# A transformer block on one core: the order of the first layer norm, the background banks of the projections, and the transfer latencies of a build-time planner

## The chip, the cores and the metric

The kernel runs on one core of one Trainium2 chip. Its engines are TensorE (PE: matmuls, and PEld: weight loads), VectorE (DVE), ScalarE (ACT), GpSimd (POOL) and SyncE (SP), which here only issues transfers. The metric is device microseconds from start to end of one execution.

## The reference

One sequence of 2048 tokens of width 640 goes through a layer norm, an attention block of 32 heads of 20, a second layer norm and a gated block without an activation function:

```python
x = A_x                                                   # 2048 x 640, bfloat16
h = x + attention(layernorm(x) @ wqkv) @ wo               # 32 heads, Dh = 20, softmax over 2048 keys
n = layernorm(h)
h2 = h + ((n @ w_gate) * (n @ w_up)) @ w_down             # gate and up 640 -> 1728, down 1728 -> 640
```

Only the inputs `A_x`, `A_wqkv`, `A_wo`, `B_w_gate`, `B_w_up`, `B_w_down` are read; `B_x` is not used.

## The kernel before

**Tiles.** Tokens are 16 tiles of 128, in four blocks `b` of 512. Heads come in eight groups `g` of four; the heads of a group stand at 32-row steps of the array. Queries come in five chunks `ci` (`CHUNKS`: three of 512, two of 256). The unit of attention is one score bank: 128 keys by 512 queries of one head, with an exponential of it. There are 2048 such units, 64 for a group in a chunk of 512.

**A score bank's way.** `rows_into` (L989) computes scores from `KTt` and `QTt`. ScalarE takes three banks at a time from `SA` into `EA`, or two from `SB` into `EB` (L1064). VectorE takes a single bank from `D0` or `D1` into an integer tile `Y` (L1089), from which two more tiles come on VectorE (L1099) and a third on GpSimd (L1097); the four are bit patterns whose sum stands for the exponential. `emit_piece` (L1140) multiplies all of these with the values `VX` into the one accumulator bank `ACC`. When a group's 64 units are through, `close_group` copies `ACC` to `acs` (L1169), and the sums travel by four small transfers: `dscr<-acs`, `dn<-dscr`, a reciprocal on VectorE (L1173), `rscr<-rn`, and `bc<-rscr`, which spreads them over the partitions; GpSimd multiplies (L1198), and the result goes to `ON`.

**First layer norm.** `ln_block` calls `layer_norm` for block 0 (two halves of two tiles), then for blocks 1, 2 and 3. Blocks 0, 2 and 3 take their statistics on VectorE (L425, L427); block 1 takes them on ScalarE (L412: sums, L417: squares). Then two small ScalarE operations give the root (L431 and L432), VectorE takes the reciprocal (L433) and normalises (L450) into one of four tiles `t`. Blocks 0 and 1 are transposed on TensorE, with a copy to `LT` (in the tensor `R`); blocks 2 and 3 by DMA transposes (L466).

**Projections.** All other matmuls are background jobs: each holds one bank, and an `evac` operation empties it. Keys and queries of groups 0 and 1 are written by `direct_proj` straight to `KTt` and `QTt`. Those of groups 2 to 7 are computed densely, 120 features by 512 tokens a job (`dense`), copied to one of four tiles `QD` (in the tensors `HH` and `L`), written to DRAM (`kscr`, `qscr`), and read back to 32-row steps (`KTt<-kscr`, 512 KB, and `QT<-qscr`, 128 KB). There are four feature tiles `i`, each with four key jobs and one query job for the first chunk. Group 2 needs tile 0, group 3 tiles 0 and 1, group 5 tile 2, group 6 tiles 2 and 3. `v_proj` computes values, 160 features (two groups) by 128 tokens a job, emptied into `VX`. Later jobs are the output projection, the second layer norm and the gated block.

**What sets the order.** Everything is ordered when the program is built, by a planner with a clock of its own. Each operation has engines, a duration, a key (smaller goes first) and a latency `lat` until others see it. `try_start` gives a free engine the ready operation of smallest key; the order so found is the fixed order of that engine's instructions in the program. On the chip an engine that waits for an operand holds all behind it. Jobs have a `target`, a position in the stream of units, and are taken in the order of their targets if their operands are ready (`next_job`). `KLO` and `KHI` place the dense key and query jobs, by `g_list(64 * g_ + KLO, 64 * g_ + KHI, ...)`, with `g_` = 2, 3, 5, 6 for the four tiles. `take_bank` decides which bank a job may have: while attention runs, only one of `D0` and `D1` may hold a background job. `d_banks` gives `D` banks to VectorE's exponentials only once the last tile of `LT` is there. For a transfer the planner takes 0.6 us on SP and `DMA_LAT` until it has landed; only the first loads have a model with sizes (`load`).

Of the kernel before, what the change touches and what calls it, by code (L numbers as in the profile page):

```python
# [17 lines left out]
P = 128  # L18
# [13 lines left out]
LNPE = 2  # L32
LNACT = (1,)
GD = 2
CHUNKS = [(0, 512), (512, 512), (1024, 512), (1536, 256), (1792, 256)]
# [22 lines left out]
LAT = 0.12  # L58
DMA_LAT = 2.1
SWITCH = 0.105  # L60
# [81 lines left out]
def kernel(  # L142
# [200 lines left out]

    def dma(o, i, key, deps=(), dur=0.6, lat=DMA_LAT):
        return add("SP", dur, lambda e: nc.sync.dma_start(o, i), key, deps, lat=lat)

    with tc.manual_schedule():
# [6 lines left out]
        free["DVE"] = 1.5  # L354
        free["POOL"] = 6.0
        kdma = [0]

# [3 lines left out]

        landed = [0.0]

        def load(o, i, kb):

            def hook(t, end, e):
                landed[0] = max(landed[0], end + 1.4) + kb / 330.0
                op.lat = landed[0] - end
            op = dma(o, i, nk())
            op.hook = hook  # L370
            return op

# [11 lines left out]
        load_x(0, 0, 2)  # L384
        load_x(0, 2, 4)
        load_w("Q0", 0, 172)
        load_w("K0", 640, 812)
        load_x(1, 0, 4)
        load_w("V0", 1280, 1440)
# [4 lines left out]
        load_w("Q", 172, 640)  # L394
        wo_ops = [dma(WO[:, :, :], A_wo.rearrange("(c p) d -> p c d", p=P), 5000)]

# [4 lines left out]
        def layer_norm(tiles, key, tdeps, dst_of, tr_key, on_pe, front=False, on_act=False):  # L401
# [6 lines left out]
            if on_act:  # L408

                js = EA[0][:, 0:D]  # L410
                deps = ([prev] if prev is not None else [])
                sums = [add("ACT", 0.75, lambda e, i=i: nc.scalar.activation(js, tiles[i], ACT.Copy, accum_out=f4[:, 0, i:i + 1]),  # L412
                            (-1,), deps + [tdeps[i]]) for i in range(n)]
                ng = add("ACT", 0.2, lambda e: nc.scalar.mul(f4[:, 3, 0:n], f4[:, 0, 0:n], -1.0 / D), (-1,), sums)
                mean = add("DVE", 0.08, lambda e: nc.vector.tensor_scalar(mv[:, 0:n, 0], f4[:, 0, 0:n], scalar1=1.0 / D, scalar2=None,
                                                                         op0=ALU.mult), (key, n), sums)
                aggs = [mean] + [add("ACT", 0.75, lambda e, i=i: nc.scalar.activation(  # L417
                    js, tiles[i], ACT.Square, bias=f4[:, 3, i:i + 1], accum_out=mv[:, i, 1:2]), (-1,), [ng]) for i in range(n)]
                o2 = add("DVE", 0.08, lambda e: nc.vector.tensor_scalar(b4[:, 2, 0:n], mv[:, 0:n, 1], scalar1=1.0 / D, scalar2=EPS_B,
                                                                        op0=ALU.mult, op1=ALU.add), (key, n), aggs)  # L420
            else:
                aggs = []
                for i in range(n):
                    deps = [tdeps[i]] + ([prev] if prev is not None else [])
                    halves_ = [add("DVE", 0.41, lambda e, i=i, c=c: nc.vector.bn_stats(  # L425
                        st[:, i, c, :], tiles[i][:, c * 320:(c + 1) * 320]), (key, i), deps) for c in range(2)]
                    aggs.append(add("DVE", 0.13, lambda e, i=i: nc.vector.bn_aggr(mv[:, i, :], st[:, i, :, :]),  # L427
                                    (key, i, 1), halves_))
                o2 = add("DVE", 0.08, lambda e: nc.vector.tensor_scalar(b4[:, 2, 0:n], mv[:, 0:n, 1], scalar1=EPS_B, scalar2=None,
                                                                        op0=ALU.add), (key, n), aggs)  # L430
# [12 lines left out]
            for i in range(n):  # L443
# [5 lines left out]
                def fn(e, i=i, slot=slot):  # L449
                    nc.vector.tensor_scalar(slot["t"][1][:], tiles[i], scalar1=mv[:, i, 0:1], scalar2=f4[:, 2, i:i + 1],  # L450
                                            op0=ALU.subtract, op1=ALU.mult)
                a = add("DVE", 0.26, fn, (key, i, 2), [o6], lock=True, hook=hook, gate=lambda: bool(t6_free))
                if on_pe:
                    def evac(bank, pm, i=i, slot=slot):
                        release_later(now[0] + 0.3, lambda: t6_free.append(slot["t"]))
                        one_done(now[0])
                        src = bank.bitcast(BF16)[:, 0:D].rearrange("p (c k) -> p c k", c=KT)
                        return add(both(), c_psum(D), lambda e: copy_on(e, dst_of(i), src), EVK, [pm])
                    mms = [("T", c, slot) for c in range(KT)]
                    jb = make_job(mms, [a], evac, "D", front=front)  # L460
                    outs.append(jb.out)
                else:
                    def sent(t, end, e, slot=slot):
                        release_later(end + 2.2, lambda: t6_free.append(slot["t"]))
                        one_done(end)
                    outs.append(add("SP", 1.5, lambda e, i=i, slot=slot: nc.sync.dma_start_transpose(dst_of(i), slot["t"][1][:]),  # L466
                                    tr_key + i, [a], hook=sent, lat=2.2))
# [68 lines left out]
        def v_proj(p, t):  # L536
# [6 lines left out]
            def evac(bank, pm):  # L543
                o = VX[:, t, 8 * p * VS:(8 * p + 8) * VS].rearrange("p (h e) -> p h e", e=VS)[:, :, 0:Dh]
                return add(both(), c_psum(160), lambda e: copy_on(e, o, bank[:, 0:160].rearrange("p (h e) -> p h e", e=Dh)),
                           EVK, [pm])
            return make_job(mms, [wl["V" if p else "V0"], lt_ops[t]], evac)
# [4 lines left out]
        def dense(wname, col, w, b, dst):  # L552
# [6 lines left out]
            def evac(bank, pm):  # L559
# [3 lines left out]
                ev = add(both(), c_psum(512), lambda e: copy_on(e, QD[k][0:w, :], bank[0:w, :]), EVK, deps)  # L563
                d = dma(dst, QD[k][0:w, :], 6, [ev])
                qd_busy[k] = d
                after([d], lambda: finish(st, now[0]))
                return ev
            make_job(mms, [wl[wname], wl[wname + "0"]] + lt_ops[4 * b:4 * b + 4], evac)
            return st
# [29 lines left out]

        KLO, KHI, VLO, VHI = -120, -60, -60, 0  # L600

# [51 lines left out]
        def pad(scr, heads, c0, c1, key):  # L653

            z = GSt[0:96, 0:512]
            z = bass.AP(tensor=z.tensor, offset=z.offset, ap=[z.ap[0], [0, heads * 12 // 96], z.ap[1]])
            return dma(scr[:, c0:c1].rearrange("(h r) c -> h r c", r=32)[:, Dh:32, :], z, key, lt_ops, dur=1.4)

        zk = [pad(kscr, 4 * (NG - GD), b * 512, b * 512 + 512, 300) for b in range(4)]
        zq = [pad(qscr[b], H, 0, 512, 301 if b == 0 else 1000) for b in range(4)]  # L660
        for g in range(GD, NG):
            deps = [kst[i, b] for i in tiles_of(g, ktiles) for b in range(4)]
            op = dma(KTt[:, g, :], kscr[(g - GD) * P:(g - GD + 1) * P, :], 5, deps + zk)
            for b in range(4):
                kj[g, b] = [op]
        rows_done = {(ci, g): Mark() for ci in range(len(CHUNKS)) for g in range(NG)}
        for ci in range(len(CHUNKS)):
            q0, cw = CHUNKS[ci]
            b, off = q0 // 512, q0 % 512
            for g in range(NG):  # L670
# [4 lines left out]
                else:  # L675
                    deps = [qst[b, ft] for ft in tiles_of(g, qtiles)] + [rows_done[ci - 1, g]]
                qj[ci, g] = [dma(QTt[:, g, 0:cw], qscr[b][g * P:(g + 1) * P, off:off + cw],
                                 5 if ci == 0 else 7, deps + [zq[b]])]

# [3 lines left out]

        def weight(o, i, lat):

            op = dma(o, i, 1200, wq_prev, lat=lat)
            wq_prev[:] = [Mark()]
# [5 lines left out]
        for f0 in range(0, NF, 3):  # L693
            c0, c1 = f0 * P, min(f0 * P + 3 * P, FF)
            gl = [weight(W_[:, :, c0:c1], A_[:, c0:c1].rearrange("(c p) f -> p c f", p=P), 2.0 + 1.6)
                  for W_, A_ in ((WG, B_w_gate), (WU, B_w_up))]
            gl_ops += [gl] * 3
        wd_ops = [weight(WD[:, f0:f0 + 2, :], B_w_down[f0 * P:(f0 + 2) * P, :].rearrange("(f p) d -> p f d", p=P), 3.5)
                  for f0 in (0, 2)]

        wq_prev[:] = lt_ops
        for f0 in (4, 7, 10):
            wd_ops.append(weight(WD[:, f0:f0 + 3, :], B_w_down[f0 * P:(f0 + 3) * P, :].rearrange("(f p) d -> p f d", p=P), 3.6))
        wd_ops.append(weight(WD[0:64, 13, :], B_w_down[13 * P:FF, :], 2.5))

# [9 lines left out]
        def chunk_jobs(ci):  # L715
            q0, cw = CHUNKS[ci]
            wo_left = [2 * (cw // P)]
            for half in range(cw // 256):
# [3 lines left out]
                for tt in pair:  # L722
# [3 lines left out]
                    def xhook(t, end, e, xs=xs):  # L726
                        xs["t"] = t6_get()
                    row = q0 + tt * P
                    xop = add("SP", 0.6, lambda e, xs=xs, row=row: nc.sync.dma_start(xs["t"][1][:], x2d[row:row + P, :]),
                              1300 + ci, [mu_mark[ci, 4]], hook=xhook, gate=lambda: len(t6_free) > 1, lat=DMA_LAT)  # L730
                    for hf in range(2):
# [422 lines left out]
        def close_group(ci, g, end):  # L1154
# [15 lines left out]
            n = cw // 32  # L1170
            d1 = dma(dscr[d][0, 0:4 * cw].rearrange("(a q) -> a q", a=4), a[Dh:P:32, 0:cw], 10, [ev] + ([ds_use[d]] if ds_use[d] is not None else []))
            d2 = dma(DN[d][:, 0:n], dscr[d][0, 0:4 * cw].rearrange("(b c) -> b c", c=n), 10, [d1])
            rc = add("DVE", 0.07 + 0.0064 * n, lambda e: nc.vector.reciprocal(RN[d][:, 0:n], DN[d][:, 0:n]), (-2,), [d2])  # L1173
            d3 = dma(rscr[d][0, 0:4 * cw].rearrange("(b c) -> b c", c=n), RN[d][:, 0:n], 10, [rc])
            ds_use[d] = d3
            bdeps = [d3] + ([bc_use[0]] if bc_use[0] is not None else [])
            src = rscr[d][0:1, 0:4 * cw]
            bsrc = bass.AP(tensor=src.tensor, offset=src.offset, ap=[[cw, 4], [0, 32], [1, cw]])
            d4 = [dma(BC[0][:, 0:cw], bsrc, 10, bdeps)]

# [20 lines left out]
            def out_of(p0, f, m):  # L1201
                return add("SP", 0.6, lambda e: nc.sync.dma_start(ON[f % P:f % P + m, on_of[ci, f // P], 0:cw], o[p0:p0 + m, 0:cw]),  # L1202
                           (10,), [mu], lat=DMA_LAT)
# [16 lines left out]
        def take_bank():  # L1220
            bgs = sum(u == "bg" for u in bank_use["D"])
            for i in range(2):
                if bank_use["D"][i] is None and (bgs == 0 or not attn["started"] or attn["over"]):
                    return ("D", i)
# [311 lines left out]
```

The softmax here doesn't subtract the row's maximum and nothing guards it: scores larger than these inputs give would overflow.

## Time and profile before

| | |
|---|---|
| time | 892.97 us, median of 3 (891.44 to 893.55) |
| span of the profiled execution | 890.7 us |
| PE busy | 818.2 us (92%) |
| ACT busy | 763.0 us (86%) |
| DVE busy | 738.7 us (83%) |
| POOL busy | 347.8 us (39%) |
| first exponential on ACT starts | 24.10 us |
| last score, then only the rest of the gated block | about 820 us, to 890.7 us |

An engine's busy time includes its pipelined instructions, so a PE at 92% is not at its peak. Read the shares by stage: in the long middle three engines are busy nine tenths of the time or more, and an idle stretch of one of them means something only if the others have no work either. Times in the text are from the span's start.

### The profile page before, as it was taken

How to read it: one execution, taken by the hardware profiler on the slowest of the kernel's cores; microseconds unless marked ns; L12 is line 12 of the kernel's file. 1: busy time of each engine (PE TensorE's matmuls, PEld its weight loads, DVE VectorE, ACT ScalarE, POOL GpSimd, SP SyncE). 2: the span in 40 equal slices, each digit the busy share in tenths (PEclk: the TensorE clock that was granted, in tenths of full speed). 3: DMA queues.
4: the chain of work that ended last, by engine and by line, in shares of the span. 5: the costliest groups of instructions: out<-in, count | busy, mean ns of one | idle time of the engine just before them, and what ended most of it. 6: DMA issues, size and time to landing. Idle time of an engine off the chain costs nothing.

```text
span 890.7 us, 34291 instructions
## 1 busy us (share of the span) xinstructions
PE 818.2 (92%) x14496; PEld 394.4 (44%) x14496; DVE 738.7 (83%) x1987; ACT 763.0 (86%) x715; POOL 347.8 (39%) x516
## 2 busy tenths in 40 slices
PE   3998889979999899999999999999889999998988
PEld 2333334332333344444323444444355655655856
DVE  5587769879899989899999898988899998898343
ACT  5787779979998899999989999999899999998211
POOL 1023324435434444444554434434454544443100
PEclk9699799989999999999979999999899999999999
DMA  8463121222224431110101001010011111101100
GB/s 266 51 168 111 37 88 49 68 86 58 74 60 120 107 87 38 41 47 25 39 19 43 22 21 50 22 46 24 23 41 38 27 40 40 29 13 42 41 15 15
DMA packets 70441, 49.64 MB, mean 56 GB/s; under 512 B 33616, under 2 KB 66352, under 8 KB 70288
## 3 DMA queue, kind: packets, MB, share of 16 engines
q1 hardware_dynamic: 70288, 47.46, 19.7%
q8 instruction: 113, 1.85, 0.9%
q14 instruction: 40, 0.33, 0.1%
HBM read 30.88 MB, written 10.32 MB: 46 GB/s over the span
## 4 chain that ended last, share of the span: by engine, by line
PE 58%; DVE 21%; DMA 9%; ACT 5%; issue 4%; SPq 2%; POOL 1%; DVEq 0%; POOLq 0%; ACTq 0%
PE D L1313 20%; PE ACC L1140 16%; DVE Y L1089 8%; PE SA L989 6%; DVE Y L1099 6%; PE D L1290 6%; PE SB L989 5%; PE D L989 4%; ACT EA L1064 2%; DMA dn<-dscr 2%; DMA bc<-rscr 2%; SPq L1202 2%; ACT EB L1064 2%; DMA QT<-qscr 1%; DVE gs L323 1%
## 5 line engine op out<-in xcount | busy, mean ns | idle before, releaser
L1064 ACT ACTIVATE EA<-SA 128x1536 bf16<-128x1536 f32 x319 | 462.4, 1449 | 37.4 <-PE SA L989 17.6
L1097 POOL TENSOR_SCALAR Y<-Y 128x512 uint16<-128x512 uint16 x463 | 300.5, 649 | 406.2 <-DVE Y L1099 286.5
L1089 DVE TENSOR_SCALAR Y<-D 128x512 uint16<-128x512 f32 x463 | 315.1, 684 | 58.5 <-PE D L989 22.4
L1064 ACT ACTIVATE EB<-SB 128x1024 bf16<-128x1024 f32 x316 | 324.7, 1028 | 22.0 <-PE SB L989 12.1
L1140 PE MATMUL ACC<-Y,VX 128*32 128x512 bf16 (+1 forms) x2348 | 265.8, 344 | 10.2 <-DVE acs L1169 5.6
L1099 DVE TENSOR_SCALAR Y<-Y 128x512 uint16<-128x512 uint16 x926 | 258.6, 324 | 4.9 <-DVE Y L1089 0.5
L1140 PE MATMUL ACC<-EA,VX 128*32 128x512 bf16 (+1 forms) x1185 | 220.4, 349 | 1.4 <-ACT EA L1064 1.1
L989 PE MATMUL D<-QT,KTt 20*128 20x512 bf16 (+1 forms) x587 | 177.7, 342 | 11.5 <-DVE Y L1089 9.1
L1140 PE MATMUL ACC<-EB,VX 128*32 128x512 bf16 (+1 forms) x788 | 177.0, 349 | 0.0
L989 PEld LDWEIGHTS <-KTt 20*128 20x128 bf16 x2560 | 74.5, 92 | 227.4 <-issue 215.8
L1313 PEld LDWEIGHTS <-R 128*32 128x32 bf16 x5350 | 127.9, 98 | 97.1 <-issue 80.1
L1140 PEld LDWEIGHTS <-VX 128*32 128x32 bf16 x4321 | 119.5, 97 | 103.1 <-issue 82.8
L989 PE MATMUL SA<-QT,KTt 20*128 20x512 bf16 (+1 forms) x1185 | 132.9, 348 | 13.3 <-ACT EA L1064 7.7
L989 PE MATMUL SB<-QT,KTt 20*128 20x512 bf16 (+1 forms) x788 | 130.7, 348 | 1.3 <-ACT EB L1064 0.8
L1313 PE MATMUL D<-L,R 128*32 128x256 bf16 x3240 | 127.9, 274 | 3.7 <-DVE HH L823 1.7
L1313 PE MATMUL D<-R 128*32 128x160 bf16 (+1 forms) x2110 | 114.0, 314 | 5.6 <-DVE VX L323 3.1
L1198 POOL TENSOR_TENSOR os<-acs,bc 128x512 bf16<-128x512 f32 (+1 forms) x40 | 42.6, 1065 | 85.4 <-DMA bc<-rscr 37.2
L823 DVE TENSOR_TENSOR HH<-D,gs 128x256 bf16<-128x256 f32 x112 | 46.8, 417 | 21.3 <-ACT gs L321 20.6
L1313 PE MATMUL D<-R,HH 128*32 128x320 bf16 x1176 | 60.1, 301 | 1.4 <-DVE HH L823 1.0
L1313 PEld LDWEIGHTS <-HH 128*32 128x32 bf16 x1176 | 30.2, 96 | 21.2 <-issue 15.9
L321 ACT CAST gs<-D 128x256 bf16<-128x256 f32 (+1 forms) x28 | 10.4, 372 | 32.5 <-PE D L1290 32.5
L323 DVE CAST gs<-D 128x256 bf16<-128x256 f32 x84 | 34.6, 412 | 1.5 <-PE D L1313 1.1
(68 smaller groups left out, 350.5 us busy)
## 6 DMA issues: line engine op xcount, KB each, us to landing
bc<-rscr SPq DMA_DIRECT2D x24, 256.0 KB
KTt<-kscr SPq DMA_DIRECT2D x6, 512.0 KB
QT<-qscr SPq DMA_DIRECT2D x22, 128.0 KB
t<-in_A_x_dram SPq DMA_DIRECT2D x16, 160.0 KB
out_dram<-t SPq DMA_DIRECT2D x16, 160.0 KB
bc<-rscr SPq DMA_DIRECT2D x16, 128.0 KB
R<-in_B_w_gate_dram SPq DMA_DIRECT2D x4, 480.0 KB
R<-in_B_w_up_dram SPq DMA_DIRECT2D x4, 480.0 KB
```

The source lines that it names most:

```text
L323: nc.vector.tensor_copy(o, i)
L823: mu = add("DVE", c_psum(256), lambda e: nc.vector.tensor_tensor(HH[0:M, f, :], bank[0:M, 256:512], GS[k][0:M, :], ALU.mult), EVK, mdeps)
L989: nc.tensor.matmul(bank[:, n * cw:(n + 1) * cw], lhsT=KTt[32 * j:32 * j + Dh, g, kt * P:(kt + 1) * P], rhs=QTt[32 * j:32 * j + Dh, g, 0:cw ...
L1064: nc.scalar.activation(st["e"][eslot["i"]][:, 0:n * 512], src[:, 0:n * 512], ACT.Exp, scale=SCALE)
L1089: p_ = add("DVE", c_psum(512), lambda e: nc.vector.tensor_scalar(YT[ys[0]][:, :], bank, scalar1=EXP_A, scalar2=EXP_B, op0=ALU.mult, op1=AL ...
L1097: nc.gpsimd.tensor_scalar(o, i_, scalar1=float(d), scalar2=1.0, op0=ALU.add, op1=ALU.mult)
L1099: nc.vector.tensor_scalar(o, i_, scalar1=float(d), scalar2=None, op0=ALU.add)
L1140: nc.tensor.matmul(ACC[32 * j:32 * j + 32, 0:cw], lhsT=VX[:, kt, h * VS:h * VS + 32], rhs=ap, start=(n == 0), stop=last, tile_position=(0, ...
L1198: mu = add("POOL", 0.1 + 2.3e-3 * cw, lambda e: nc.gpsimd.tensor_tensor(o[:, 0:cw], a[:, 0:cw], BC[0][:, 0:cw], ALU.mult), (0,), d4 + os_u ...
L1202: return add("SP", 0.6, lambda e: nc.sync.dma_start(ON[f % P:f % P + m, on_of[ci, f // P], 0:cw], o[p0:p0 + m, 0:cw]), (10,), [mu], lat=DM ...
L1290: nc.tensor.matmul(bank[0:M, c0:c1], lhsT=lhs(0, M), rhs=rhs(), start=first, stop=last, skip_group_check=True)
L1313: nc.tensor.matmul(bank[32 * j:32 * j + 32, c0:c1], lhsT=lhs(32 * j, 32 * j + 32), rhs=rhs(), start=first, stop=last, tile_position=(0, 32 ...
```

## The change

The planner's constants and some of its rules change; what is computed does not. The parts:

1. *Layer norm by need*: the ScalarE statistics of block 1 had key −1, ahead of all else on ScalarE. They get `STK` = 0.4, behind the root of block 0 and the emptying of banks (key 0), ahead of exponentials (key 1). The load of block 1 is issued before the first weights. Durations of these operations are set to longer values.
2. *Two background banks*: until the last tile of `LT` is planned as done, both `D` banks may hold background jobs.
3. *Keys and queries sooner*: `KLO, KHI` goes from −120, −60 to −150, −100. Dense jobs now wait for all 16 tiles of `LT`, not only for the four of their block.
4. *Down projection weights*: nine loads of one tile (160 KB) in place of three of three tiles (480 KB), the other loads as before.
5. *Transfers in the planner*: each transfer has its own issue time and a latency that grows with its size and with what is already under way, at 330 KB/us. The wide `bc` gets 1.8 + cw/200, that is 4.36 us for 512 columns; small transfers get about 1.4 in place of 2.1.

```diff
-DMA_LAT = 2.1
+DMA_LAT = 1.5
...
+    def dma(o, i, key, deps=(), dur=0.6, lat=1.25, kb=0):
+        def hook(t, end, e):
+            landed[0] = max(landed[0], end + 0.3) + kb / 330.0
+            op.lat = max(lat, landed[0] - end + 1.1)
...
         load_x(0, 2, 4)
+        load_x(1, 0, 4)
         load_w("Q0", 0, 172)
         load_w("K0", 640, 812)
-        load_x(1, 0, 4)
         load_w("V0", 1280, 1440)
...
-                sums = [add("ACT", 0.75, ... ACT.Copy ..., (-1,), ...
+                sums = [add("ACT", 0.87, ... ACT.Copy ..., (STK,), ...
...
-                a = add("DVE", 0.26, fn, (key, i, 2), [o6], lock=True, ...
+                a = add("DVE", 0.36, fn, (key, i, 2), [o6], lock=True, ...
...
-            make_job(mms, [wl[wname], wl[wname + "0"]] + lt_ops[4 * b:4 * b + 4], evac)
+            make_job(mms, [wl[wname], wl[wname + "0"]] + lt_ops, evac)
...
-        KLO, KHI, VLO, VHI = -120, -60, -60, 0
+        KLO, KHI, VLO, VHI = -150, -100, -60, 0
...
-            op = dma(KTt[:, g, :], kscr[(g - GD) * P:(g - GD + 1) * P, :], 5, deps + zk)
+            op = dma(KTt[:, g, :], kscr[(g - GD) * P:(g - GD + 1) * P, :], 5, deps + zk, dur=0.35, kb=512, lat=3.5)
...
-        for f0 in (4, 7, 10):
-            wd_ops.append(weight(WD[:, f0:f0 + 3, :], ...
+        for f0 in range(4, NF - 1):
+            wd_ops.append(weight(WD[:, f0, :], B_w_down[f0 * P:(f0 + 1) * P, :], 164))
...
-            d2 = dma(DN[d][:, 0:n], ..., 10, [d1])
+            d2 = dma(DN[d][:, 0:n], ..., 10, [d1], dur=0.33, kb=8)
...
-            d4 = [dma(BC[0][:, 0:cw], bsrc, 10, bdeps)]
+            d4 = [dma(BC[0][:, 0:cw], bsrc, 10, bdeps, lat=1.8 + cw / 200.0)]
...
-                if bank_use["D"][i] is None and (bgs == 0 or not attn["started"] or attn["over"]):
+                if bank_use["D"][i] is None and (bgs == 0 or not attn["started"] or attn["over"] or lt_ops[NT - 1].done is None):
```

Since the planner decides every order, these edits also move instructions far from them: on each engine nearly the whole list differs.

## The prediction

> **What bounds the kernel now.** I read the page's 40 slices first, then ScalarE's waits, the stages around its longest ones, the chain of waits there, and the first 25 us in order of time.
>
> ScalarE does over three quarters of the exponentials, so its waits mark where attention stands still. Columns: line, what it waited for, us in total, times, longest.
>
> ```profile
> ACT lf L431 <- DVE lb L429: 18.5, 2, 12.8
> ACT EA L1064 <- PE SA L989: 17.6, 36, 1.8
> ACT EA L1064 <- PE D L989: 16.1, 6, 8.6
> ACT EB L1064 <- PE D L989: 7.7, 8, 4.2
> ACT EA L412 <- DMA R<-in_A_x_dram: 1.9, 1, 1.9
> ```
>
> The third and fourth rows hide three holes: 8.6 us (ends 91.7), 5.5 (ends 124.2) and 4.2 (ends 186.9). The stages (us from start, length, busy of PE, PEld, DVE, ACT, POOL, granted clock, DMA share, GB/s) show what was idle beside ScalarE:
>
> ```profile
> 24.00:46.00 22.00, 20.15 (x277) 8.14 (x274) 12.60 (x38) 15.80 (x18) 0.00 (x0) 0.69 0.45 53
> 46.00:82.00 36.00, 35.15 (x558) 12.05 (x560) 30.49 (x75) 34.43 (x30) 13.05 (x20) 1.00 0.52 146
> 82.00:92.00 10.00, 5.44 (x109) 2.46 (x109) 2.94 (x7) 1.40 (x3) 0.99 (x2) 0.92 0.39 112
> 92.00:102.00 10.00, 9.79 (x132) 3.94 (x134) 7.35 (x21) 7.34 (x7) 2.76 (x5) 0.56 0.13 40
> 116.00:125.00 9.00, 6.71 (x144) 2.87 (x132) 3.37 (x8) 3.50 (x4) 0.00 (x0) 1.00 0.28 92
> 180.00:191.00 11.00, 6.77 (x130) 3.13 (x122) 5.65 (x17) 5.57 (x6) 2.60 (x5) 0.69 0.22 66
> 191.00:820.00 629.00, 597.37 (x11310) 279.20 (x11307) 574.54 (x1548) 601.44 (x532) 289.83 (x425) 0.98 0.17 44
> ```
>
> In 191 to 820 PE, DVE and ACT are busy 95, 91 and 96%: three engines share the bound, and reordering finds little. In the holes all are idle, PE for 4.6, 2.3 and 4.2 us; after the first, PE runs at half clock. The chain of waits at the first hole (start, us, what), and the start in order of time:
>
> ```profile
> 84.06 2.85 DMA qscr<-HH
> 86.91 0.02 issue
> 86.93 4.09 DMA QT<-qscr
> 91.02 0.04 issue
> 91.06 0.61 PE SA L989 x3
> ```
>
> ```profile
> 7.74 0.34 ACT L431 ACTIVATE lf<-lb 128x2 f32<-128x2 bf16 x2 [5.71 <-DVE lb L429]
> 10.00 0.74 ACT L412 ACTIVATE EA<-R 128x640 bf16<-128x640 bf16 x1 [1.92 <-DMA R<-in_A_x_dram]
> 13.31 0.19 ACT L432 ACTIVATE lb<-lf 128x2 bf16<-128x2 f32 x1
> 13.73 0.80 DVE L450 TENSOR_SCALAR t<-R,lmv,lf 128x640 bf16<-128x640 bf16 x2
> 24.10 1.45 ACT L1064 ACTIVATE EA<-SA 128x1536 bf16<-128x1536 f32 x1 [0.69 <-PE SA L989]
> ```
>
> Group 2 waits for its queries' trip through DRAM; the second hole is the same for group 3 (`qscr<-HH` 2.91, `QT<-qscr` 3.93). In the third, `qscr<-L` took 4.20 us behind two 512 KB `KTt` loads, `dn<-dscr` stood behind `QT` on SP, and VectorE waited 4.45 us at the reciprocal. At the start, block 0's half-finished root (L431 at 7.74, L432 at 13.31) stands behind block 1's four sums, whose tokens landed at 10.00.
>
> **What the Trainium skill says.** "TensorE: Matmul & The Clock Gate", Part 1: after an idle window of about 3.4 us PE gets half clock, and needs a busy one to get it back. The trace agrees in part: PE stood from 87.5 to 91.06, and half clock held from 91.5 to 101.7, longer than one window. The same page's table of specifications: ScalarE and VectorE are strict first-in first-out; 13.31 above shows it. "DMA: Bandwidth & Descriptors", Anatomy of one DMA: most of a fixed 2 us is the receipt from the target memory, which no reordering shortens; 2.85 us for a 120 KB write agrees.
>
> **The change part by part.**
>
> *Layer norm.* The loads moved 1974 KB by 9.0 us and 2247 KB by 10.0, when block 1 (1750 KB with all ahead of it) had landed, so it trails by some 490. With 440 KB less ahead it needs 1800, reached at 8.3 on the same curve; 7.5 is the other end, as small weight packets (221 to 265 GB/s at 5 to 7 us, against 386) no longer stand in between. In the new ScalarE order two of the four sums still stand ahead of L431: 2 × 0.86 us, to 9.2 to 10.0; L431 and L432 for both halves add about 0.65, so L450 starts at 10.2 to 11.0 against 13.73: 3.1 us sooner. The fourth L450 now stands ahead of the first `VX` copy (it started at 17.63 behind one), but the `QT` and `KTt` copies stand on VectorE behind five statistics (2.7 us), and 16 matmuls of the next job come ahead of the first score. First exponential: about 19.2 against 24.10. Not all is kept. Block 1's root still follows its squares; the DMA transposes of blocks 2 and 3 (5.9 and 6.2 us) follow each other as before, so the last tile of `LT` comes perhaps 2.6 us sooner than 46.3, and I count three more units (37 against 34 ahead of the first `D` score), worth 3 × 0.37: 3.7, say **−4** (2 to 6).
>
> *Two background banks and keys sooner.* The PE order gives the units already scored when each feature tile's last dense job ends:
>
> ```
> tile (needed by)       before   after
> 0 (group 2, unit 128)   123      97
> 1 (group 3, unit 192)   198     142
> 2 (group 5, unit 320)   274     246
> 3 (group 6, unit 384)   325     332
> ```
>
> From the last dense matmul (82.97) to the score (91.06) took 8.1 us. A unit takes 0.37 us (some 1610 of L1064 and L1089 in the timeline from 200 to 800), so tile 0 has 31 × 0.37 = 11.5 us, and tile 1 18.5. On SP `KTt` and `QT` of group 2 now stand well ahead of group 1's `dscr<-acs`, `QT` of groups 3 and 4 before group 2's. Both holes should close. What it brings is PE's idle time, not ScalarE's: the bank matmuls done within the holes have to be done elsewhere, and beside them PE is 95 to 98% busy. So −4.6 and −2.3. The half clock at 91.5 to 101.7 should go with its idle stretch: 10.2 us, up to 5 of PE; PE is not alone the bound, so −2.5, near ScalarE's idle 2.7 at 92 to 102.
> The price: 588 background matmuls against 465 before unit 64, the 100 of tile 0 among them. They are moved, not added, and groups 2 and 3 have 280 and 220 against 348 and 316. Values of groups 2 and 3 come 17 units later (145 against 128 for the first), so their products lag; 30 units fit in `EA`, `EB` and `Y`, which hides that.
>
> *Latencies.* In the third hole's place `qscr` now precedes the two `KTt` loads, and the planner counts their bytes, so VectorE's reciprocal is put later: −3 of PE's 4.2, and −1.5 of the half clock after it. Elsewhere `dn` has real latencies of 1.76 (`dscr` to `dn` issue) and about 1.7 us, 3.5 together against 5.4 planned before and 3.75 now: just enough, and `bc` took up to 5.2 against 2.7 before and 4.96 now. So GpSimd's 37.2 us of waits for `bc` shrink, but GpSimd is 39% busy: 0. I charge +1 for reciprocals that are now tight.
>
> *Down projection weights.* Six more issues on SP at 0.4 to 0.7 us; the bytes are the same, DMA was half idle at 46 to 82: 0.
>
> *End.* After the last score there are 188 matmuls of 320 columns against 174, one job more: 14 × 0.134 = **+1.9**. VectorE takes 467 units for 463: 0.
>
> Sum: −4 − 4.6 − 2.3 − 2.5 − 3 − 1.5 + 1 + 1.9 = −15, from 892.97: **878**.
>
> **The rivals.**
> *All of ScalarE's idle time comes back.* −5 − 8.6 − 5.5 − 4.2 − 2.7 + 1.9 = −24: 869. For it: in 140 to 180 attention kept 55 units in 20 us with projections beside it. Against: PE at 95%.
> *The early stretch becomes the bound.* At 24 to 46 PE is busy 20.2 of 22 at clock 0.69, and the change puts 6 us more of dense jobs there. Then the start keeps −2, and of the 13.9 for holes, half clock and reciprocal 6 to 8 come back: 892.97 − 2 − 8 + 2 = 885.
> *Planned too tightly: slower.* The reciprocal stands 1.65 us earlier in VectorE's order; VectorE already waited there 12 times, 11.6 us. If each of 40 waits the whole 1.65, that is 66 us, of which VectorE's share of the chain (21%) is 14; with no hole closed, the start's −4 and the end's +2: 905, or 894 to 900 if some of the holes close. Against: 3.5 measured is below 3.75.
>
> **How the numbers follow.** Forecast (872 to 884) 0.6; all back 0.13; early bound 0.16; slower 0.08; no difference 0.03. Faster 0.89. The range reaches into the cases on both sides, 866 to 888; left out are slower, no difference and the fringe of the first rival, under 0.2.
>
> **What would show it.** Right: the first exponential at 18 to 21 us; no wait of ScalarE over 3 us between 60 and 200; no half clock around 92 to 102; the last score near 803. Wrong: ScalarE's holes gone but as much idle in many waits below 2 us; longer waits of VectorE for `dn`; a stage 24 to 82 that carries no more units; new waits for `VX` in groups 2 and 3.

## The result and the profile after

The changed kernel takes 870.02 us (median of 4, 863.82 to 872.78) against 893.26 us for the kernel before: a ratio of 0.971 [0.963, 0.979]. That is 23 us where 15 were forecast, and inside the range. The profiled executions have spans of 890.7 and 869.4 us, so the traces account for 21.3 us. Executions of one kernel differ as well: the shortest of the changed kernel, 863.82 us, ran at a mean granted clock of 0.996, the longest, 872.78 us, at 0.982.

ScalarE's waits in the kernel after (line, what it waited for, us in total, times, longest; lines after the first edits stand three lower than before, so L1064 is now L1067):

```profile
ACT EB L1067 <- PE SB L992: 17.6, 26, 2.7
ACT EA L1067 <- PE SA L992: 16.4, 36, 2.7
ACT EA L415 <- DMA R<-in_A_x_dram: 6.4, 1, 6.4
```

Of the row of waits for a `D` bank with its 8.6 us, 0.4 us are left; no wait at an exponential exceeds 2.7 us. The stages (from:to, length, busy us of PE, PEld, DVE, ACT, POOL with counts, granted clock, DMA share, GB/s):

```profile
24.00:46.00 22.00, 19.48 (x447) 9.98 (x445) 17.35 (x53) 16.95 (x20) 1.86 (x3) 1.00 0.52 80
46.00:82.00 36.00, 31.67 (x443) 10.21 (x442) 28.88 (x69) 29.35 (x25) 13.06 (x19) 0.96 0.52 144
82.00:92.00 10.00, 9.73 (x162) 3.78 (x163) 9.02 (x24) 9.39 (x9) 3.67 (x7) 0.97 0.60 187
92.00:102.00 10.00, 8.76 (x198) 3.98 (x190) 8.26 (x26) 8.55 (x8) 3.87 (x7) 1.00 0.26 75
116.00:125.00 9.00, 9.00 (x190) 3.54 (x186) 7.83 (x23) 8.99 (x9) 3.71 (x7) 1.00 0.19 61
180.00:191.00 11.00, 10.88 (x163) 3.80 (x160) 9.67 (x28) 10.48 (x10) 5.03 (x9) 1.00 0.23 64
```

ScalarE's busy time in the three stages of the holes went from 1.40 to 9.39 us of 10, from 3.50 to 8.99 of 9, and from 5.57 to 10.48 of 11, and the granted clock is 0.97 to 1.00. But 46 to 82 got worse: 29.35 us of ScalarE where it had 34.43. A wait of 2.7 us (ends 48.59) stands behind a copy of keys on VectorE. Another of 2.7 us (ends 78.53) and a shorter one after it are a rest of the first hole, by the chain of waits (start, us, what):

```profile
68.62 7.16 DMA qscr<-HH
...
75.80 2.09 DMA QT<-qscr
```

Group 2's queries still travel too late. The write of 120 KB took 7.16 us, not 2.85: on SP a 256 KB `bc` was issued at 67.45 and the 512 KB `KTt` read at 68.14, right ahead of it. This rest lies ahead of unit 128, and 3.4 us of half clock follow it (from 79.1). The start, in order of time:

```profile
8.38 0.74 ACT L415 ACTIVATE EA<-R 128x640 bf16<-128x640 bf16 x1 [6.35 <-DMA R<-in_A_x_dram]
9.97 0.28 ACT L434 ACTIVATE lf<-lb 128x2 f32<-128x2 bf16 x2
10.19 0.30 ACT L435 ACTIVATE lb<-lf 128x2 bf16<-128x2 f32 x2
10.63 0.80 DVE L453 TENSOR_SCALAR t<-R,lmv,lf 128x640 bf16<-128x640 bf16 x2
19.65 1.45 ACT L1067 ACTIVATE EA<-SA 128x1536 bf16<-128x1536 f32 x1 [0.35 <-PE SB L992]
```

**Where the time went.** ScalarE's and VectorE's exponentials of score banks can be counted through the trace. The table gives the us between the end of the n-th and of the m-th unit, for every kernel of this study; the columns 128–160, 192–224 and 320–384 hold the three holes of before. ScalarE ends three units at a time, so a column is good to about 1 us. "Old" and "sized" are the planner's latencies, "D banks" how many may hold background jobs before `LT` is whole.

```
                 latencies D banks   0-64 64-128 128-160 160-192 192-224 224-320 320-384 384-512 512-1024 1024-2040  rest
before           old       1         58.9   24.2    23.1    12.5    17.2    36.2    27.6    49.2    191.8     379.1  70.9
after            sized     2         54.9   26.8    12.6    12.4    12.0    35.3    24.3    48.5    189.7     379.0  73.9
e1_one_bank      sized     1         52.9   23.3    24.6    11.7    11.3    36.7    23.5    46.9    189.3     382.3  72.4
e2_keys_back     sized     2         56.4   27.4    13.2    11.7    14.0    36.0    24.9    46.9    188.3     383.2  72.9
e3_ln_back       sized     2         55.6   25.1    12.0    11.9    12.5    33.4    25.6    47.7    190.9     382.2  75.7
e4_lat_back      old       2         55.1   27.6    12.1    14.0    11.0    36.8    28.6    47.3    194.8     382.9  78.2
e5_lat_only      sized     1         61.8   24.4    20.4    12.3    14.9    35.0    23.3    47.4    192.0     383.5  73.5
e6_bank_only     old       2         56.2   24.0    11.9    15.6    11.2    36.1    28.4    49.0    195.1     388.9  76.9
e7_jit_after     sized     2         56.0   28.5    11.5    15.2    11.2    34.2    25.0    51.0    192.0     380.2  70.4
e8_jit_before    old       1         55.3   23.9    24.4    12.3    16.7    35.4    27.0    51.4    196.2     382.4  81.9
e9_pe_double     sized     2         55.9   25.7    11.6    12.5    12.0    35.7    25.8    48.3    191.4     382.8  74.8
e10_chain_back   mixed     2         55.7   23.9    12.6    12.3    12.3    38.2    25.4    48.7    197.2     379.3  72.2
e11_both_first   sized     2         52.3   24.5    11.6    12.6    11.7    34.6    24.3    47.8    192.2     379.6  75.1
e12_jit_after2   sized     2         53.5   26.1    13.0    10.6    12.5    36.1    25.7    48.2    190.4     380.3  73.2
```

Before less after, by column and before rounding: 4.0 − 2.5 + 10.5 + 0.1 + 5.2 + 0.9 + 3.2 + 0.7 + 2.0 + 0.2 − 3.0 = 21.3 us. The columns of the holes are 18.9 of it, and the rest of the first hole, in units 64–128, takes 2.5 back.

### The profile page after: what moved, and what is told of

Read it like the earlier page. It is cut to its first block, busy times and chain, and to the rows that moved or that the text cites. A ratio compares the mean times of both kernels' runs of the same rounds, so it can differ in the third digit from the quotient of the medians.

```text
span 869.4 us, 34285 instructions
## 1 busy us (share of the span) xinstructions
PE 806.7 (93%) x14491; PEld 388.5 (45%) x14491; DVE 734.2 (84%) x2002; ACT 757.3 (87%) x711; POOL 353.6 (41%) x520
## 4 chain that ended last, share of the span: by engine, by line
PE 57%; DVE 20%; DMA 9%; ACT 9%; issue 3%; SPq 1%; POOL 0%; DVEq 0%; ACTq 0%
PE D L1316 20%; PE ACC L1143 15%; DVE Y L1092 7%; PE D L1293 7%; PE SA L992 6%; DVE Y L1102 6%; ACT EA L1067 5%; PE D L992 4%; PE SB L992 4%; ACT EB L1067 4%; DMA dn<-dscr 3%; DMA dscr<-acs 2%; DMA qscr<-HH 1%; DVE acs L1172 1%; DVE HH L826 1%
## 5 line engine op out<-in xcount | busy, mean ns | idle before, releaser
L1067 ACT ACTIVATE EA<-SA 128x1536 bf16<-128x1536 f32 x319 | 462.1, 1449 | 24.3 <-PE SA L992 16.4
L1100 POOL TENSOR_SCALAR Y<-Y 128x512 uint16<-128x512 uint16 x467 | 305.9, 655 | 406.9 <-DVE Y L1102 270.1
L1067 ACT ACTIVATE EB<-SB 128x1024 bf16<-128x1024 f32 x315 | 324.3, 1030 | 20.4 <-PE SB L992 17.6
L1102 DVE TENSOR_SCALAR Y<-Y 128x512 uint16<-128x512 uint16 x934 | 252.0, 316 | 3.0
L1143 PE MATMUL ACC<-EA,VX 128*32 128x512 bf16 (+1 forms) x1186 | 215.7, 343 | 1.3 <-ACT EA L1067 1.1
L1143 PE MATMUL ACC<-EB,VX 128*32 128x512 bf16 (+1 forms) x785 | 169.4, 343 | 0.3 <-ACT EB L1067 0.3
L1316 PEld LDWEIGHTS <-R 128*32 128x32 bf16 x5370 | 124.4, 96 | 95.6 <-issue 75.4
L992 PE MATMUL SB<-QT,KTt 20*128 20x512 bf16 (+1 forms) x785 | 126.1, 342 | 2.5 <-ACT EB L1067 2.1
L1316 PE MATMUL D<-R 128*32 128x160 bf16 (+1 forms) x2130 | 106.2, 301 | 5.5 <-DVE VX L325 3.0
L826 DVE TENSOR_TENSOR HH<-D,gs 128x256 bf16<-128x256 f32 x112 | 46.9, 419 | 21.9 <-ACT gs L323 21.1
L1316 PE MATMUL D<-R,HH 128*32 128x320 bf16 x1136 | 55.3, 301 | 1.8 <-DVE HH L826 1.6
L1316 PEld LDWEIGHTS <-HH 128*32 128x32 bf16 x1136 | 27.1, 96 | 22.4 <-issue 17.5
```

What stands on the lines that cost most here:

```text
L826: mu = add("DVE", c_psum(256), lambda e: nc.vector.tensor_tensor(HH[0:M, f, :], bank[0:M, 256:512], GS[k][0:M, :], ALU.mult), EVK, mdeps)
L992: nc.tensor.matmul(bank[:, n * cw:(n + 1) * cw], lhsT=KTt[32 * j:32 * j + Dh, g, kt * P:(kt + 1) * P], rhs=QTt[32 * j:32 * j + Dh, g, 0:cw ...
L1067: nc.scalar.activation(st["e"][eslot["i"]][:, 0:n * 512], src[:, 0:n * 512], ACT.Exp, scale=SCALE)
L1100: nc.gpsimd.tensor_scalar(o, i_, scalar1=float(d), scalar2=1.0, op0=ALU.add, op1=ALU.mult)
L1102: nc.vector.tensor_scalar(o, i_, scalar1=float(d), scalar2=None, op0=ALU.add)
L1143: nc.tensor.matmul(ACC[32 * j:32 * j + 32, 0:cw], lhsT=VX[:, kt, h * VS:h * VS + 32], rhs=ap, start=(n == 0), stop=last, tile_position=(0, ...
```

## The experiments

Two questions: does a closed hole return ScalarE's idle time or only PE's, and which part of the change does it? And since a planner reorders nearly everything after any edit: how much do two plans differ when nothing is meant to differ? Ratios are to before, timed beside each run; its medians there were 891 to 897 us, so totals of different runs can be compared only to within a few us.

**One background bank again** (`e1_one_bank`), all else as after:

```diff
-... or attn["over"] or lt_ops[NT - 1].done is None):
+... or attn["over"]):
```

> The changed kernel with the old bank rule: one background bank while attention runs, all else as changed. Theory A (the second background bank closes the first hole): in PE's order the last job of feature tile 0 ends at unit 128, where group 2 needs it, against 97 with two banks, so ScalarE waits about 8 us there and half clock follows: 870 + 11 = 881 us. Rival B (sized transfers in the planner close the holes): 870 to 873. Rival C (keys placed sooner by KLO close both holes): 870 to 873.

Measured 876.41 us (875.24 to 877.16), ratio to before 0.980 [0.976, 0.985]. ScalarE's waits, and the stage of the first hole:

```profile
ACT EA L1067 <- PE D L992: 11.4, 6, 8.4
```

```profile
82.00:92.00 10.00, 7.24 (x96) 2.55 (x96) 4.79 (x13) 5.04 (x5) 1.24 (x2) 0.64 0.31 89
```

The first hole is back with nearly its old length, and half clock with it; units 128–160 take 24.6 us. The second stays closed (11.3). The net loss at unit 160 is smaller, 6.6 us (100.8 for 94.2): by unit 128 this kernel is 5.4 us ahead of after. It has issued 536 background matmuls by then, against 680, and the rest of the hole doesn't stand there. In the PE order tile 0's last dense job ends after 128 units with one bank, 97 with two; tile 1's after 154, well ahead of its 192.

**Keys and queries at their old place** (`e2_keys_back`):

```diff
-        KLO, KHI, VLO, VHI = -150, -100, -60, 0
+        KLO, KHI, VLO, VHI = -120, -60, -60, 0
```

> The changed kernel with KLO, KHI back at -120, -60. In PE's order tile 0 still ends at unit 97, tile 1 at 181 instead of 142 (needed at 192). Theory A: the first hole stays closed, tile 1 has 11 units or 4 us for a trip of 8.1, so a hole of 4 to 5 us opens at group 3: 874 to 876 us. Rival C: both holes come back, 885 us. Rival B: 870 to 872.

Measured 876.88 us (872.69 to 881.23), 0.982 [0.977, 0.986]. The first hole stays closed but for its rest (2.9 us, ends 80.19); tile 0 still ends after 97 units and tile 1 after 181. In place of the 4 to 5 us expected at group 3, ScalarE waits 2.3 us there (ends 110.97) for the queries' trip (`qscr<-HH` 4.22, `QT<-qscr` 2.46), and units 192–224 take 14.0 for 12.0. So tile 0 owes its lead to the bank rule; `KLO` and `KHI` move only tile 1 and those behind it.

**The old layer norm order** (`e3_ln_back`):

```diff
-STK = 0.4
+STK = -1
...
-        load_x(1, 0, 4)
         load_w("Q0", 0, 172)
         load_w("K0", 640, 812)
+        load_x(1, 0, 4)
```

> The changed kernel with the old layer norm order: block 1's statistics ahead of all else on ScalarE (key -1) and its load behind the first weights. Theory A: the first exponential goes back from 19.7 us to about 24, nothing else: 874 to 875 us. A rival, that the early start decides what comes later (group 2's tiles in time): 880 us or more, with a hole at group 2.

Measured 874.78 us (874.12 to 882.41), 0.980 [0.975, 0.985]. The half-finished root is back (L434 at 7.89, L435 at 12.96):

```profile
7.89 0.34 ACT L434 ACTIVATE lf<-lb 128x2 f32<-128x2 bf16 x2 [5.87 <-DVE lb L432]
...
12.96 0.19 ACT L435 ACTIVATE lb<-lf 128x2 bf16<-128x2 f32 x1
```

The eighth unit is done at 26.7 us, against 23.4 after and 27.8 before: the early start is this part's. But unit 64 is done at 55.6 against 54.9, and from unit 128 (80.7 against 81.6) to 1024 (414.4 against 416.6) this kernel is ahead of after. What it loses in the whole, 2.9 us by the traces, lies behind unit 1024. The early start is not kept.

**All old latencies** (`e4_lat_back`): the rest of the change stays, and so do a few durations (0.75 us for an issue to `ON`, 1.3 for a DMA transpose).

```diff
-DMA_LAT = 1.5
+DMA_LAT = 2.1
...
-        op = add("SP", dur, lambda e: nc.sync.dma_start(o, i), key, deps, lat=lat, hook=hook)
+        return add("SP", dur if dur == 1.4 else 0.6, lambda e: nc.sync.dma_start(o, i), key, deps, lat=DMA_LAT)
```

> The changed kernel with the planner's old transfers: 0.6 us and 2.1 us for all, the old model for the first loads. In PE's order the tiles end at 97, 139, 240, 328, nearly as changed. Theory A: the holes at groups 2 and 3 stay closed; VectorE's wait for dn near 185 may come back, and GpSimd waits more for bc: 872 to 875 us. Rival B: at least half of the gain goes, 881 us or more.

Measured 887.34 us (881.86 to 893.12), 0.993 [0.989, 0.997]: 17 of the 23 us are gone. The first two holes stay closed but for the rest of the first (2.5 us, ends 76.18), the third is open (28.6). The other losses against after are 5.1 us in units 512–1024, 3.9 in 1024–2040 and 4.3 in the rest.

**Latencies alone, and the bank rule alone**, both on the kernel before: `e5_lat_only` has part 5 of the change and nothing else, `e6_bank_only` this:

```diff
-... or attn["over"]):
+... or attn["over"] or lt_ops[NT - 1].done is None):
```

> The kernel before with the sized transfers alone. In PE's order the tiles end at 123, 198, 271, 320, as before, so both holes should stay. Theory A: only the wait behind the KTt loads near 185 and GpSimd's waits for bc shrink: 886 to 891 us. Rival B (the latencies carry what e4 lost, 17 us, wherever they are applied): 876 to 880 us.

> The kernel before with the rule of two background banks alone. Tile 0 ends at unit 90 instead of 123, tile 1 at 195 (needed at 192). Theory A: the first hole closes with its half clock, some 11 us, and the second stays, a little longer: 882 us. Rival B: 890 to 893 us, since transfers planned too short leave the hole open.

`e5_lat_only`: 887.08 us (879.25 to 895.63), 0.996 [0.994, 0.999]. `e6_bank_only`: 895.21 us (891.72 to 901.76), 1.005 [1.003, 1.007]. With latencies alone the first hole stays (ScalarE's longest wait 6.8 us), the third closes (23.3). With the bank rule alone the first hole is full of work:

```profile
82.00:92.00 10.00, 10.00 (x190) 3.94 (x193) 9.39 (x28) 9.71 (x9) 3.90 (x6) 1.00 0.35 116
```

Units 128–160 fall from 23.1 to 11.9 us. That is 11.1 us, where ScalarE's idle time was 8.6 + 2.7 and PE's part, by the forecast, 4.6 + 2.5. The second hole is smaller but not gone. ScalarE waits 3.2 us (ends 103.16) for group 3's queries, one column earlier, where units 160–192 take 15.6 for 12.5:

```profile
94.72 5.85 DMA qscr<-HH
...
100.58 1.99 DMA QT<-qscr
```

By unit 224 this kernel is 17.1 us ahead of before; by unit 2040 3.4, and at the end behind. Alone, then, each of the two brings nearly nothing. The two together without the other parts were not tried.

**A planner constant moved by 2 ns** (`SWITCH`, the gap between two of PE's jobs), to see how much plans differ by chance: `e7_jit_after` and `e12_jit_after2` from after, `e8_jit_before` from before.

```diff
-SWITCH = 0.105
+SWITCH = 0.107
```

(0.103 in `e12_jit_after2`.)

> The changed kernel with the planner's time for a change of PE mode at 0.107 us instead of 0.105: a plan that differs in detail and in nothing meant. If plans of one kind differ by chance by less than 3 us, this is 867 to 873 us, and the losses of e1 to e4 are the parts'. If it is 876 us or more, chance alone makes a good part of them.

> The kernel before with the same 0.107 us. Tile 0 ends at unit 127 instead of 123, tile 1 at 198. No chance in plans: 893 us, at most 2 more for tile 0. With chance: outside 890 to 897 us.

> The changed kernel with 0.103 us for a change of mode, a second plan that differs in nothing meant. Units 512 to 2040 in 570 to 574 us, the end in 71 to 76; time 868 to 878.

`e7_jit_after` 875.65 us (869.61 to 881.98), 0.982 [0.977, 0.988]; `e12_jit_after2` 871.47 (861.6 to 876.14), 0.972 [0.958, 0.986]; `e8_jit_before` 909.54 (903.12 to 914.01), 1.020 [1.015, 1.026]. So plans around after spread by up to some 5 us, and `e12_jit_after2` isn't told apart from after. Single executions of after and of `e7_jit_after` spread as much (863.8 to 872.8, 869.6 to 882.0). A neighbour of before is 16 us slower than it, 18 against the runs of before beside it: before looks like a lucky plan of its kind, by this one neighbour. This limits what `e1_one_bank` to `e3_ln_back` say. Their 5 to 7 us in the total are no more than chance between plans; only a local step of the table that recurs in every plan of a kind can be put down to a part. The first two below do; the third is weaker, since the two kinds overlap:

- units 128–160: 20.4 to 24.6 us in the four plans with one bank, 11.5 to 13.2 in the ten with two (units 64–160, with the rest of the hole: 44.8 to 48.3 against 36.0 to 40.6);
- units 320–384: 27.0 to 28.6 in the four with old latencies, 23.3 to 25.8 in the ten others;
- units 512–1024: 191.8 to 197.2 where the latencies of the sums' way are old (five plans), 188.3 to 192.2 in the nine others; and the rest after unit 2040: 70.9 to 81.9 against 70.4 to 75.7.

**More work for PE, none for ScalarE** (`e9_pe_double`): the dense query jobs of blocks 2 and 3 run their matmuls twice, the second pass starting the sums anew, so the output stays; 180 matmuls more.

```diff
-            for c in range(KT):
+            for c in list(range(KT)) * times:
...
-... dense("Q", f, w, b, rows(qscr[b], f, w, 0, 512))
+... dense("Q", f, w, b, rows(qscr[b], f, w, 0, 512), 2 if b > 1 else 1)
```

> The changed kernel with every matmul of the twelve query jobs of token blocks 2 and 3 done twice (the second pass starts the sum anew): 180 more background matmuls, about 13 us of TensorE, mostly between units 400 and 600; nothing else is added to any engine. If TensorE is the bound (my prediction's sizing, only PE's idle time comes back), unit 640 comes 10 to 13 us later than in the changed kernel. If ScalarE and VectorE are, it comes 0 to 4 us later.

Measured 877.62 us (876.72 to 881.61), 0.985 [0.978, 0.992]: 7.6 us over after by the medians, 7.2 by the traces (by the two ratios it would be 12). In after 930 such matmuls keep PE busy for 73.5 us in all, 79 ns each, so 180 would be 14 us if PE alone set the pace. About half of that arrived, and chance between plans is nearly as large. The stretch with the added work says more. The groups of 240 to 280 us, after first (line, operation, count, busy us, mean ns, idle before):

```profile
L1316 PE MATMUL D<-WO,ON 128*32 128x320 bf16 x160 | 8.2, 301 | 0.1
...
L1316 PE MATMUL D<-R 128*32 128x512 bf16 x10 | 1.4, 381 | 0.0
```

```profile
L1316 PE MATMUL D<-R 128*32 128x512 bf16 x220 | 19.4, 382 | 0.0
...
L1316 PE MATMUL D<-WO,ON 128*32 128x320 bf16 x20 | 1.2, 303 | 0.0
```

and the stage in which units 512 to 640 run, again after first:

```profile
227.00:274.00 47.00, 41.94 (x588) 15.34 (x586) 43.46 (x112) 44.80 (x41) 21.17 (x30) 1.00 0.37 97
```

```profile
227.00:274.00 47.00, 46.38 (x627) 14.60 (x620) 39.44 (x94) 46.40 (x41) 18.97 (x29) 1.00 0.14 38
```

PE went from 89 to 99% busy, the 128 units took 46.9 us for 47.1, and unit 640 came 0.6 us later than in after, as expected for ScalarE and VectorE as the bound. But the plan displaced another job, 140 of the output projection's matmuls. Net, PE was busy for 4.4 us more, and that fitted into the 5.1 us that it had been idle. So this idle time could be filled without loss of pace; whether a PE that is 95 to 98% busy has room as well isn't shown. The loss comes later: 2.4 us by unit 1024, 6.2 by 2040.

**The old latency for the sums' way only** (`e10_chain_back`): `dscr`, `dn`, `rscr` and `bc` get 2.1 us again.

```diff
-            d4 = [dma(BC[0][:, 0:cw], bsrc, 10, bdeps, lat=1.8 + cw / 200.0)]
+            d4 = [dma(BC[0][:, 0:cw], bsrc, 10, bdeps, lat=2.1)]
```

(and the same for the other three.)

> The changed kernel with the old 2.1 us for the four transfers that close a group (dscr, dn, rscr, bc), the other transfers sized. So far units 512 to 2040 took 570 to 573 us in the plans with sized transfers (changed, e1, e2, e3, e7; 575 in e5) and 570, 579, 584, 578 in those without (before, e8, e6, e4); from there to the end 71 to 76 us against 72 to 82. Theory D (GpSimd's waits for bc, planned at 2.1 and taking 5, do it): 577 us or more and GpSimd waits for bc above 30 us in all, time 877 to 882. If the key and query transfers do it: 570 to 574, time 870 to 875.

Measured 879.11 us (877.55 to 885.91), 0.987 [0.980, 0.995]. The third hole stays closed (25.4), so it depends on the latencies of other transfers than these four. Units 512 to 2040 take 576.5 us, just under the 577 of theory D. The loss against after lies in units 224–1024: 2.9, 1.1, 0.2 and 7.5 us. GpSimd's waits for `bc` double, from the first of these to the second (after, then `e10_chain_back`):

```profile
POOL os L1201 <- DMA bc<-rscr: 20.9, 17, 3.0
```

```profile
POOL os L1201 <- DMA bc<-rscr: 41.7, 16, 9.7
```

They are 18.5 to 26.4 us in all plans with sized latencies, and 37.2, 51.9, 65.4 and 65.8 in before, `e8_jit_before`, `e6_bank_only` and `e4_lat_back`. Yet the one long wait that falls among the units 224–1024 of `e10_chain_back` held up nobody, by the timeline and the stage around it:

```profile
301.45 1.36 POOL L1201 TENSOR_TENSOR os<-acs,bc 128x512 bf16<-128x512 f32 x1 [4.45 <-DMA bc<-rscr]
```

```profile
297.00:303.00 6.00, 6.00 (x127) 2.90 (x124) 5.81 (x15) 5.97 (x6) 1.47 (x2) 1.00 0.52 126
```

GpSimd stood for 4.45 us while ScalarE was busy for 5.97 of 6 and VectorE for 5.81. So these waits go with slower plans, but that they make them slower is not shown. One loss in these units can be placed elsewhere, on VectorE and then PE:

```profile
280.06 3.13 DVE L1102 TENSOR_SCALAR Y<-Y 128x512 uint16<-128x512 uint16 x9
283.12 0.68 DVE L1172 COPY acs<-ACC 128x512 f32<-128x512 f32 x1
283.85 0.62 PE L1143 MATMUL ACC<-Y,VX 128*32 128x512 bf16 x4 [2.26 <-DVE acs L1172]
```

PE stood 2.26 us for the copy of `ACC`, which stood behind nine tiles `Y` on VectorE; 6.8 us of half clock followed (from 283.0), and ScalarE waited up to 2.6 us. What had put VectorE behind is not shown.

**Both rough edges of after** (`e11_both_first`): block 1's sums wait for block 0's root, and a tile's query job goes ahead of its four key jobs.

```diff
-                deps = ([prev] if prev is not None else [])
+                deps = ([prev] if prev is not None else []) + roots
...
-[A(k_dense, i, b) for b in range(4)] + [A(q_dense0, i)])
+[A(q_dense0, i)] + [A(k_dense, i, b) for b in range(4)])
```

> The changed kernel with block 0's root ahead of block 1's sums on ScalarE, and each feature tile's query job ahead of its four key jobs. The first normalisation should start at 8.6 to 9 us instead of 10.63, the first exponential 1 to 2 us sooner, and the query write should no longer land 7.2 us after its issue behind bc and KTt, so that the wait for QT (3.1 us near 75) goes: 4 to 5 us less, 865 us, give or take the 5 us that plans differ by chance.

Measured 867.42 us (864.82 to 871.01), 0.973 [0.966, 0.980]. The start, in order of time:

```profile
8.01 0.33 ACT L436 ACTIVATE lb<-lf 128x2 bf16<-128x2 f32 x2
8.44 0.80 DVE L455 TENSOR_SCALAR t<-R,lmv,lf 128x640 bf16<-128x640 bf16 x2
18.07 0.58 ACT L323 CAST KTt<-D 128x512 bf16<-128x512 f32 x1 [0.16 <-PE D L1318]
20.46 1.45 ACT L1069 ACTIVATE EA<-SA 128x1536 bf16<-128x1536 f32 x1
```

The normalisation starts at 8.44 for 10.63, and the first exponential *later*, at 20.46 for 19.65: the copy of the keys and the exponential now stand on ScalarE behind block 1's squares. Unit 64 comes 2.6 us sooner all the same. The wait for group 2's queries is gone (no wait at an exponential exceeds 2.1 us), unit 128 is done at 76.7 for 81.6, unit 512 at 219.4 for 226.8. Of these 7.4 us 4.4 are left at unit 2040 and 3.2 in the span, which is within chance between plans. It is the fastest here by its median, but not told apart from after.

## Why the prediction was right

The direction, the place and the first mechanism were right: the two holes closed but for a rest of the first ahead of unit 128, and the half clock at 92 to 102 us is gone. Not every step of the sum was right, and some of the agreement is luck. The sum, by its steps (a minus is a gain):

| step | forecast | in the trace | |
|---|---|---|---|
| layer norm | −4 | −4.0 at unit 64 | only in part this part's |
| hole 1 and its half clock | −4.6 − 2.5 | −10.5 in units 128–160, +2.5 in 64–128 by its rest | near as a sum |
| hole 2 | −2.3 | −5.2 | too small |
| third hole and its half clock | −3 − 1.5 | −3.2 | near |
| reciprocals | +1 | VectorE's wait for `dn` 11.6 to 12.8 | small, as forecast |
| end | +1.9 | +3.0 | near |
| everything else | 0 | −3.9 | not forecast |

*Hole sizes.* The term that the columns contradict is "What it brings is PE's idle time, not ScalarE's", with its ground that the holes' matmuls must go elsewhere, beside a PE that is 95 to 98% busy. The second hole returned 5.2 us, where ScalarE's idle time was 5.5 and PE's 2.3. The first returned 10.5 us in its column (ScalarE's 8.6 + 2.7, PE's 4.6 + 2.5), 8.0 with its rest. Where no such rest stands, in `e6_bank_only` and `e11_both_first`, units 64–160 took 36.0 and 36.1 us against 47.3: ScalarE's idle time came back in full. One pair speaks for the forecast, though. `e1_one_bank` lost 12.0 us in the hole's column, but only 6.6 net at unit 160, near PE's 7.1. Between before and `e6_bank_only` the net at unit 160 is 14.1. So within the holes ScalarE's idle time returns; what the moved matmuls cost elsewhere stays open.

`e9_pe_double` doesn't settle that. The Trainium skill, "Perfetto Trace Analysis", Identifying the Most-Contended Engine, says that matmul busy time doesn't measure how near PE is to its limit, because matmuls are pipelined, and that weight-load busy time says more. In this case a stage with PE shown as 89% busy took 46.38 busy us in place of 41.94 with the units as fast, and weight loads filled only 15 of the 47 us; no stage with PE at 95 to 98% was loaded further.

The rival "all of ScalarE's idle time comes back" came nearer (869), but in part by luck: it put 21.0 us on the three holes and their half clock, of which 16.4 came, 5 on the start, and nothing on the 3.9 us of "everything else".

*Layer norm.* Every time in its working came out: L415's load at 8.38 (7.5 to 8.3 forecast), L453 at 10.63 (10.2 to 11.0), the first exponential at 19.65 (about 19.2). The step that fails is "I count three more units", that is, that a lead in units lasts. `e3_ln_back`, with the old order and the rest of the change, is 0.7 us behind after at unit 64 and ahead of it from unit 128. So that 4.0 us were met at unit 64 is mostly luck: `e8_jit_before`, too, with the old order and no other part, needs 55.3 us for 64 units, against 58.9 in before and 54.9 in after.

*The two parts taken together.* "Two background banks and keys sooner" was costed as one. The experiments part them: the first hole is the bank rule's. For the second the early keys are what closes it, as far as these runs show: with two banks and the old place of the keys, ScalarE still waits for group 3's queries, 3.2 us in `e6_bank_only` and 2.3 in `e2_keys_back`; with early keys and one bank (`e1_one_bank`) units 160–224 take 23.0 us, the least of all. This is less clean than the first: these units take 29.0 and 29.8 us with neither and old latencies, 25.7 to 27.2 in `e2_keys_back`, `e6_bank_only` and `e5_lat_only`, but 26.5 also in `e7_jit_after`, with early keys. Early keys alone were not tried.

*The residual hole.* "Both holes should close" rested on PE's order, in which tile 0 ends 31 units ahead. The keys came in time; the query job comes last of its five, and its write met a 256 KB and a 512 KB transfer. That ScalarE's wait there is the query job's is borne out by `e11_both_first`, though that run changes the layer norm too. The prediction took 2.85 us for it from before, where nothing large stood ahead of it.

*Latencies.* They were costed at the third hole alone (−4.5); 3.2 came, and the runs tie it to them. That they also shelter the long middle and the end isn't in the sum, since it compares two plans and before looks like a good one: the middle from unit 512 to 2040 came out nearly equal (570.9 and 568.7 us). It shows with the neighbours: three other plans with all old latencies need 577.7 to 584.0 us there, the sized ones 568.7 to 575.5. The three also have more half clock there, 31 to 38 us against 10 to 27 in the eleven others; whether as cause or as consequence is not shown. GpSimd's waits were put at 0, which the stage at 297 to 303 us bears out for one of them; why the middle slows isn't settled.

*Down projection weights.* Costed at 0; not tried alone. Two of the 160 KB loads were issued at 65.68 and 69.41 us, around the slow query write, so a share of its 7.16 us may be theirs. Not tried either are small edits of the change that its list leaves out, such as the planner's times for the copies to `LT` and for the DMA transposes.

*Half clock.* The prediction placed it at 91.5 to 101.7 us; it runs from 90.5 to 100.7, and its length is as said. That it follows an idle window is too narrow, as the last section shows.

## What to carry to other kernels

In the stretch of a hole, the idle time of the engine that carries the stage's work can come back in full; what has been moved to fill it may have to be paid elsewhere, so compare the clock at a milestone behind both. A busy share leaves open how much more fits: add work and look at the pace, and check what the added work displaced. Where a planner or scheduler places everything, move one harmless constant by a hair, before and after: that spread tells which differences between totals may be put down to an edit, and a table of the time between milestones finds what is real inside it. An early start pays only if the next thing that everybody waits for comes sooner too.

## What was not expected of the hardware

- A 120 KB write to DRAM that took 2.85 us in before took 7.16 us with 256 KB and 512 KB issued within 1.2 us ahead of it.
- One idle stretch of 3.5 us on PE (before, 87.55 to 91.06) came with 10.2 us of half clock (90.5 to 100.7), and all half-clock stretches of both traces are multiples of 3.41 us. The Trainium skill, "TensorE: Matmul & The Clock Gate", Part 1, gives that length for a free-running window, and at least one busy window for the way back; here it took three.
- 2 ns in a constant of the planner changed the time by 16 us (before) and by 1.5 and 5.6 us (after), of which the 1.5 lie within the spread of single executions.
- Half clock needed no idle window of that length. In the 3.41 us ahead of each of the 13 falls to half clock of both traces (before and after), PE was 2 to 81% busy by its matmuls. Ahead of the third hole's fall it was 2.17 us of 3.41, or 64% (before; columns as in the stages, the granted clock third from the end):

```profile
179.22:182.63 3.41, 2.17 (x59) 1.04 (x48) 1.28 (x4) 3.41 (x3) 1.34 (x2) 1.00 0.43 142
182.64:189.46 6.82, 3.84 (x59) 1.80 (x62) 4.00 (x13) 1.84 (x3) 1.65 (x3) 0.50 0.16 47
```

Nor is the share alone a rule: other such windows in these traces, 56 to 77% busy, were followed by full clock.
